# Local attention feeding a PReLU network: the first q in one load, later q and k behind it, and one weight split issued later

## The chip, the cores and the metric

The kernel runs on one core of a Trainium2 chip. The metric is the device time of one execution in microseconds (us); lower is better. The core has a matrix engine (PE; its weight loads are shown apart as PEld), a vector engine (DVE), a scalar engine (ACT), a general engine (POOL) and a queue engine (SP). Transfers are started by instructions on SP, ACT and POOL; the profile writes SPq, ACTq and POOLq where an engine only issues one. Each engine takes its instructions in a fixed order, and an instruction that waits holds up all that stand behind it on its engine.

## What is computed

Attention within chunks of 64 tokens, then a two-layer network with a PReLU, all in float32. The reference, cut to its core:

```python
# q, k, v: (8, 8, 576, 64); chunks of 64 tokens
scores = scale * np.matmul(q_c, k_c.transpose(0, 1, 2, 4, 3))
scores = scores - np.max(scores, axis=-1, keepdims=True)
attn = np.exp(scores)
attn = attn / (np.sum(attn, axis=-1, keepdims=True) + 1e-09)
out = np.matmul(attn, v_c)
# x: (4608, 512) from out; w_in: (512, 2048); w_out: (2048, 512)
h = x @ w_in
g = np.maximum(h, 0.0) + alpha * np.minimum(h, 0.0)
return (g @ w_out).astype(np.float32)
```

## The kernel before

**Tiling.** The 4608 tokens are 36 sub-blocks of 128 tokens (two chunks of 64, all eight heads). Four sub-blocks make a block of 512 tokens, so there are nine blocks. The first three blocks go through the network directly ("plain"); the other six go in three pairs through a scheme with seven half-size products in place of eight, whose combined weights are computed meanwhile and kept in DRAM.

**Number format.** Each float32 operand of the network is held as a high and a low part, and each product takes three passes: high by high, low by high, high by low. Weights reach the chip as raw words. `split_weight` (L120) turns one piece of a weight, 128 x 512, into its two parts: two instructions on ACT (the absolute value at L130, the rounded high part at L134) and seven on DVE (L131, L132, L133, L135, L136, L137, L138). There are 16 pieces of each weight; `wi[f]` belongs to the first layer and `wo[f]` to the second. `prepare(f)` (L141) splits both.

**Attention of an early sub-block s (the first eight).** It has three stages, called by `attend`:

- Stage 0: `attn_scores` multiplies q by a block-diagonal k on PE (L180); `attn_softmax` takes the maximum on DVE (L210), scales it (L211), forms eight exponentials on ACT, one for each head (L214, each an ACTIVATE and a read of its sum), and then on DVE the sum's reciprocal (L216, L217) and the product (L218).
- Stage 1: `attn_transpose` transposes the probabilities on PE (L242), and ACT copies them into a block-diagonal tile in two halves (L249, L250).
- Stage 2: `attn_values` multiplies by v on PE (L260), and `attn_x` writes the high part of the network's input x on ACT (L292) and its low part on DVE (L293).

Below, S, T and V with a number stand for the scores, the transposes and the values product of that sub-block, counted from 0.

**Network step.** `ffn_in` runs 12 matmuls of the first layer (L311) into one of two banks `ps_h`; `prelu` follows with L301 and L302 on ACT and L303 on DVE; L323 on ACT and L324 on DVE split the result into `gh` and `gl`; `ffn_out` runs 12 matmuls of the second layer (L336). The first three steps work on block 0 with weights 0, 1 and 2, the next nine on block 1 from weight 0 on, since the weights arrive one after the other. When a block's turn is over, `store` copies its sums out (L366).

**Order.** The instructions of the early part are put in order by a scheduler that estimates times; the kernel only gives priorities (`high_priority`) and orderings (`issue_after`: nothing inside may stand ahead of the instruction named). A small change to the program can therefore move instructions far behind it. From the 21st step on PE's own order is fixed by the program.

**Start.** `fetch("wi", 0)` loads the first weight piece on SP. `first_q(s, n, queue)` (L415) loads q of n sub-blocks, `first_k(s, other)` (L422) loads the two halves of a k, one on SP and one on the queue named, and `first_v` loads v of two sub-blocks. Several of the tiles carry names of weights (wi, wo), since they lie in rooms that later hold weights.

Of the kernel before, what the change touches and what calls it, by code (L numbers as in the profile page):

```python
# [18 lines left out]
def bits(pattern):  # L19
    return struct.unpack("f", struct.pack("I", pattern))[0]  # L20
# [7 lines left out]
def tile_local_attention_prelu_ffn(  # L28
# [12 lines left out]
    nc = tc.nc  # L41
# [31 lines left out]
    def f32(t):  # L73
        return t.bitcast(F32)
# [34 lines left out]
    wi, wo = {}, {}  # L109
# [4 lines left out]
    def fetch(side, f):  # L114
        name = ("raw", "raw", "more")[fetched[0] % 3]
        fetched[0] += 1
        raws[side, f] = stage.tile([P, 512], I64, name=name, bufs=2 if name == "raw" else 1)
        nc.sync.dma_start(out=raws[side, f], in_=(w_in if side == "wi" else w_out)[:, f])

    def split_weight(side, f):  # L120
        if (side, f) not in raws:
            fetch(side, f)
        raw = raws.pop((side, f))
        words = raw.bitcast(U32).rearrange("p (n two) -> p two n", two=2)
        low, high = words[:, 0], words[:, 1]
        t1 = stage.tile([P, 512], U32, name="t1")
        t3 = stage.tile([P, 512], U32, name="t3", bufs=1)
        w = const.tile([P, 2, 512], F32R, name=f"{side}{f}")
        hi, lo = w[:, 0], w[:, 1]
        nc.scalar.activation(f32(t1), f32(high), AF.Abs)  # L130
        nc.vector.tensor_scalar(f32(t1), f32(t1), bits(0x38000000), bits(0x47EFFFFF), op0=ALU.max, op1=ALU.min)  # L131
        nc.vector.tensor_scalar(t1, t1, 3, 0x3FFFF000, op0=ALU.logical_shift_left, op1=ALU.bitwise_and)  # L132
        nc.vector.scalar_tensor_tensor(t1, in0=high, scalar=0xC0000000, in1=t1, op0=ALU.bitwise_and, op1=ALU.bitwise_or)  # L133
        nc.scalar.copy(hi, f32(t1))  # L134
        nc.vector.tensor_scalar(t3, high, 0x1FF, 15, op0=ALU.bitwise_and, op1=ALU.logical_shift_left)  # L135
        nc.vector.scalar_tensor_tensor(t3, in0=low, scalar=17, in1=t3, op0=ALU.logical_shift_right, op1=ALU.bitwise_or)  # L136
        nc.vector.tensor_scalar(t1, t1, 0xFF800000, None, op0=ALU.bitwise_and)  # L137
        nc.vector.scalar_tensor_tensor(lo, in0=t3, scalar=2.0 ** -35, in1=f32(t1), op0=ALU.mult, op1=ALU.mult)  # L138
        return w

    def prepare(f, behind=None):  # L141
        with tc.issue_after(behind.ins) if behind else nullcontext():
            wi[f] = split_weight("wi", f)
            wo[f] = split_weight("wo", f)
# [7 lines left out]
    stages = {}  # L152
# [19 lines left out]
    def attn_scores(s):  # L172
        q_sb, kb, _ = qkv[s]
        early = s < EARLY
        if early:

            sc = attn_psum(s, 0)
            for h in range(H):
                par, hp = h % 2, h // 2
                pe(nc.tensor.matmul(  # L180
                    sc[par * C:(par + 1) * C, hp * P:(hp + 1) * P],
                    lhsT=q_sb[:, h, :],
                    rhs=kb[:, :, h],
                    start=True, stop=True,
                ))
            sc3 = sc.rearrange("p (g k) -> p g k", k=C)
        else:


            for hp in range(NP):  # L190
                for c in range(2):
                    for par in range(2):
                        rows = slice(par * C, (par + 1) * C)
                        pe(nc.tensor.matmul(  # L194
                            att[par][c * C:(c + 1) * C, (NP + hp) * C:(NP + hp + 1) * C],
                            lhsT=q_sb[rows, 2 * hp + c],
                            rhs=kb[rows, 2 * hp + c],
                            start=True, stop=True,
                        ))
            sc3 = [a[:, NP * C:].rearrange("p (g k) -> p g k", k=C) for a in att]  # L200
        return sc3

    def attn_softmax(s, sc3):
        early = s < EARLY
        mx = soft.tile([P, H, 1], F32, name="mx", bufs=2)
        pr = prs[s // 2 % 2][:, s % 2] if early else soft.tile([P, H, C], F32, name="pr")
        sm = soft.tile([P, H, 1], F32, name="sm", bufs=2)
        parts = [(slice(0, H), sc3)] if early else [(slice(b * NP, (b + 1) * NP), sc3[b]) for b in range(2)]
        for at, part in parts:
            nc.vector.tensor_reduce(mx[:, at], part, axis=AX.X, op=ALU.max)  # L210
        scaled = nc.vector.tensor_scalar(mx, mx, -SCALE, None, op0=ALU.mult)  # L211
        for g in range(H):
            one = sc3[:, g] if early else sc3[g // NP][:, g % NP]
            last = nc.scalar.activation(pr[:, g], one, AF.Exp, bias=mx[:, g], scale=SCALE, accum_out=sm[:, g])  # L214
        stages["softmax"] = scaled, last
        nc.vector.tensor_scalar(sm, sm, 1e-9, None, op0=ALU.add)  # L216
        nc.vector.reciprocal(sm, sm)  # L217
        nc.vector.tensor_tensor(pr, pr, sm.broadcast_to([P, H, C]), op=ALU.mult)  # L218
        probs[s] = pr
# [167 lines left out]
    def attend(part, s):  # L387
        with tc.high_priority(offset=HIGH):
            if part == 0:
                attn_softmax(s, attn_scores(s))  # L390
            elif part == 1:
                attn_transpose(s) if s < EARLY else attn_blocks(s)
            else:
                attn_x(s, attn_values(s))
# [20 lines left out]
    def first_q(s, n, queue):  # L415

        q_sb = qs[s // 2 % 2][:, s % 2:s % 2 + n]
        queue.dma_start(out=q_sb, in_=qT[:, s:s + n].rearrange("p s (h t) -> p s h t", t=C))
        for i in range(n):
            qkv[s + i] = [q_sb[:, i], kbds[(s + i) % NBD], None]  # L420

    def first_k(s, other):  # L422

        for c, queue in enumerate((nc.sync, other)):
            rows = slice(c * C, (c + 1) * C)
            queue.dma_start(out=kbds[s % NBD][rows, c], in_=kT[rows, s].rearrange("p (h t) -> p h t", t=C))
# [6 lines left out]
            qkv[s + i][2] = v_sb[:, i]  # L433

    fetch("wi", 0)
    first_q(0, 1, nc.scalar)
    first_k(0, nc.scalar)
    first_q(1, 1, nc.scalar)
    first_k(1, nc.scalar)
    first_q(2, 2, nc.sync)  # L440
    first_k(2, nc.sync)
    first_v(0)
    fetch("wo", 0)
# [1 line left out]
    first_v(2)  # L445
    fetch("wi", 1)
    nc.gpsimd.dma_start(out=alpha_sb, in_=alpha)
    prepare(0)
    ready = 1
    for i in range(SPB + 2):  # L450
        for st in range(2, -1, -1):
            if 0 <= i - st < SPB:
                attend(st, i - st)
                if st == 2 and i % 2:
                    first_q(i + 1, 2, nc.sync)
                    first_k(i + 1, nc.sync)
                    first_k(i + 2, nc.sync)
                    first_v(i + 1)
# [452 lines left out]
```

## Time and profile before

| | us |
|---|---|
| median of three runs | 839.68 |
| the three runs | 834.14, 841.08, 839.68 |
| the profiled execution, whole time | 837.25 |
| its span in the trace | 835.5 |
| PE busy in the span | 806.1 |
| first matmul of the network starts at | 37.54 |

The profiled execution's whole time is 1.75 us longer than its span. Times of day in the rows below count from the start of the span. A row of a timeline has start, duration, engine, line, operation, output tile, input tiles, shapes and count, and in square brackets the time for which the engine had stood idle and what ended that. In a timeline a run of instructions of one kind is merged; a score product of eight matmuls in the program shows as 16 there, since each is run as two.

### The profile page before, as it was taken

Reading aid. Unit: us, or ns where it says so; the run is one execution under the profiler, and the core shown is the slowest. Engines: PE = TensorE matmul, PEld = TensorE weight load, DVE = VectorE, ACT = ScalarE, POOL = GpSimd, SP = SyncE. Lnnn points to the kernel's source line nnn. Section 1 sums busy time; section 2 is a strip of 40 time slices with the busy share of each in tenths; the row PEclk is TensorE's granted clock in tenths of the full one; section 3 lists DMA queues with packets and bytes.
Section 4 is the critical chain, followed back from the end, with each engine's and each line's share of the span. In section 5 each row is a group of like instructions: output and inputs, shape, how many; then the busy total and the mean of one; then the engine's idle time right before and its main releaser. Section 6 shows DMA issues by size and latency. Waiting matters only on the chain.

```text
span 835.5 us, 15368 instructions
## 1 busy us (share of the span) xinstructions
PE 806.1 (96%) x5248; PEld 644.8 (77%) x5248; DVE 671.0 (80%) x1268; ACT 542.8 (65%) x1392; POOL 215.7 (26%) x340
## 2 busy tenths in 40 slices
PE   4799999999989899999999999999999999999998
PEld 3577888777768678787788788787887888888886
DVE  5899999979769888677688996777789966568875
ACT  5985666657666576677876555687765546566452
POOL 4006223224324432111112242111122422111232
PEclk9999999999999899999999999999999999999999
DMA  9629777656687868687876799786557995555788
GB/s 277 215 78 343 236 248 267 192 159 205 207 212 238 222 202 287 223 270 260 260 248 208 225 241 335 261 268 207 187 199 234 250 296 188 187 191 188 237 228 231
DMA packets 73966, 192.40 MB, mean 230 GB/s; under 512 B 11664, under 2 KB 19104, under 8 KB 73760
## 3 DMA queue, kind: packets, MB, share of 16 engines
q0 software_dynamic: 38272, 127.43, 48.7%
q1 hardware_dynamic: 27248, 48.91, 18.5%
q10 hardware_dynamic: 8368, 15.08, 5.6%
q8 instruction: 42, 0.69, 0.3%
q14 instruction: 36, 0.29, 0.1%
HBM read 135.27 MB, written 42.99 MB: 213 GB/s over the span
## 4 chain that ended last, share of the span: by engine, by line
PE 83%; ACT 4%; DMA 4%; DVE 3%; SPq 3%; issue 2%; ACTq 0%; POOL 0%; DVEq 0%
PE ps_o L623 19%; PE ps_o L756 15%; PE ps_h L756 12%; PE ps_h L311 12%; PE ps_o L336 12%; PE ps_h L623 9%; SPq L232 3%; DMA pT<-t 2%; PE ps_a L272 2%; PE ps_a L194 1%; DMA wi<-kT 1%; ACT wo L214 1%; ACT pr L214 1%; DMA wo_a<-raw 1%; ACT wi L214 1%
## 5 line engine op out<-in xcount | busy, mean ns | idle before, releaser
L336 PE MATMUL ps_o<-wo,gh 128*128 128x512 f32 x384 | 114.7, 397 | 1.2 <-ACT g L366 1.2
L311 PE MATMUL ps_h<-xh,wi 128*128 128x512 f32 x384 | 107.4, 402 | 1.8 <-DVE g L303 1.2
L311 PEld LDWEIGHTS ps_h<-xh,wi 128*128 128x128 f32 x384 | 72.0, 190 | 19.9 <-DVE g L303 1.7
L336 PEld LDWEIGHTS ps_o<-wo,gh 128*128 128x128 f32 x384 | 71.5, 188 | 19.1 <-ACT g L366 1.6
L214 ACT ACTIVATE pr<-ps_a,mx 128x64 f32<-128x64 f32 x224 | 67.3, 328 | 25.2 <-DVE mx L211 23.1
L336 PE MATMUL ps_o<-wo,gl 128*128 128x512 f32 x192 | 69.3, 396 | 0.1
L623 PE MATMUL ps_o<-wi,raw 128*128 128x512 f32 x171 | 67.9, 397 | 0.0
L623 PE MATMUL ps_o<-wo,raw 128*128 128x512 f32 x171 | 67.8, 396 | 0.0
L311 PE MATMUL ps_h<-xl,wi 128*128 128x512 f32 x192 | 53.4, 400 | 0.0
L561 POOL DMA_DIRECT2D raw<-wi_a x42 | 22.4, 532 | 106.4 <-PE ps_o L623 60.6
L214 ACT ACTIVATION_READ_ACCUMULATOR pr<-ps_a,mx 128x1 f32 x224 | 49.5, 221 | 0.0
L323 ACT CAST gh<-g 128x512 fp32r<-128x512 f32 x48 | 29.9, 622 | 28.9 <-DVE g L303 22.9
L301 ACT ACTIVATE wo<-gh 128x512 f32<-128x512 f32 x24 | 15.2, 634 | 50.4 <-DVE gh L646 50.4
L579 ACT CAST gh<-wi 128x512 fp32r<-128x512 f32 x45 | 28.1, 625 | 25.3 <-PE ps_o L756 10.3
L561 POOL DMA_DIRECT2D raw<-wo_a x42 | 22.4, 532 | 84.9 <-PE ps_o L756 44.0
L311 PEld LDWEIGHTS ps_h<-xl,wi 128*128 128x128 f32 x192 | 36.6, 191 | 8.7
L301 ACT ACTIVATE g<-ps_h 128x512 f32<-128x512 f32 x48 | 29.4, 613 | 21.1 <-PE ps_h L311 20.8
L336 PEld LDWEIGHTS ps_o<-wo,gl 128*128 128x128 f32 x192 | 35.9, 188 | 9.3 <-DVE gl L324 0.5
L623 PE MATMUL ps_o<-wi,wo 128*128 128x512 f32 x99 | 39.3, 397 | 0.0
L623 PE MATMUL ps_o<-wo,wo 128*128 128x512 f32 x99 | 39.1, 395 | 0.0
L623 PEld LDWEIGHTS ps_o<-wo,raw 128*128 128x128 f32 x171 | 32.2, 188 | 7.7
L623 PEld LDWEIGHTS ps_o<-wi,raw 128*128 128x128 f32 x171 | 32.1, 188 | 7.6
(251 smaller groups left out, 2285.3 us busy)
## 6 DMA issues: line engine op xcount, KB each, us to landing
raw<-wi_a POOLq DMA_DIRECT2D x42, 512.0 KB, 4.7
raw<-wo_a POOLq DMA_DIRECT2D x42, 512.0 KB, 4.7
wi<-wi_a POOLq DMA_DIRECT2D x21, 512.0 KB, 4.5
wo<-wi_a POOLq DMA_DIRECT2D x21, 512.0 KB, 4.7
wi<-wo_a POOLq DMA_DIRECT2D x21, 512.0 KB, 4.6
wo<-wo_a POOLq DMA_DIRECT2D x21, 512.0 KB, 5.1
v_sb<-v SPq DMA_DIRECT2D x28, 256.0 KB, 4.8
pT<-t SPq DMA_DIRECT2D x224, 32.0 KB, 4.0
```

Of the source, the lines that this page charges most:

```text
L194: pe(nc.tensor.matmul(att[par][c * C:(c + 1) * C, (NP + hp) * C:(NP + hp + 1) * C], lhsT=q_sb[rows, 2 * hp + c], rhs=kb[rows, 2 * hp + c], ...
L214: last = nc.scalar.activation(pr[:, g], one, AF.Exp, bias=mx[:, g], scale=SCALE, accum_out=sm[:, g])
L232: nc.sync.dma_start(out=pT[dst, i].rearrange("p h t -> p (h t)"), in_=tb[src, j].rearrange("p h t -> p (h t)"),)
L272: pe(nc.tensor.matmul(att[c][par * C:(par + 1) * C, hp * C:(hp + 1) * C], lhsT=v_sb[rows, h * C:(h + 1) * C], rhs=p[rows, :, par * NP + hp ...
L301: nc.scalar.activation(g, h, AF.Relu, scale=-1.0)
L311: pe(nc.tensor.matmul(hps, lhsT=wi[f][:, l, k * P:(k + 1) * P], rhs=xx[:, k], start=(i == 0 and k == 0), stop=(i == 2 and k == NK - 1),))
L323: nc.scalar.copy(gh, g)
L336: pe(nc.tensor.matmul(o, lhsT=a[:, ts], rhs=wo[f][:, l], start=(f == first and i == 0), stop=(f == last and i == 2),))
L561: streamed[0] = nc.gpsimd.dma_start(out=f32(t), in_=units[side][n])
L579: hi = nc.scalar.copy(t_hi, t)
L623: pe(nc.tensor.matmul(ps, lhsT=w[:, l, k * P:(k + 1) * P], rhs=xx[:, xl], start=first and at == 0, stop=at == n - 1, skip_group_check=not ...
L756: pe(nc.tensor.matmul(ps[m], lhsT=w[:, l, m * P:(m + 1) * P], rhs=xx, start=i != 6 and j == 0 and n == 0, stop=j == JF - 1 and n == 2, ski ...
```

## The change

Three calls at the start and one in the loop over the first block:

- The q of sub-blocks 0 and 1 come in one load of 512 KB on ACT's queue, ahead of both k's; before, there was a load of 256 KB, the first k's half, the second 256 KB and the second k's half.
- The q of sub-blocks 2 and 3 goes to ACT's queue behind these, and no longer to SP's queue ahead of the third k.
- `prepare(0)` is taken apart: `wi[0]` is split where it was, and `wo[0]` is split inside the loop, after the attention stage 0 of sub-block 2, and not ahead of the scaling of that sub-block's maximum.

```diff
     fetch("wi", 0)
-    first_q(0, 1, nc.scalar)
+    first_q(0, 2, nc.scalar)
     first_k(0, nc.scalar)
-    first_q(1, 1, nc.scalar)
     first_k(1, nc.scalar)
-    first_q(2, 2, nc.sync)
+    first_q(2, 2, nc.scalar)
     first_k(2, nc.sync)
     first_v(0)
     fetch("wo", 0)
...
-    prepare(0)
+    wi[0] = split_weight("wi", 0)
     ready = 1
     for i in range(SPB + 2):
         for st in range(2, -1, -1):
             if 0 <= i - st < SPB:
                 attend(st, i - st)
+                if st == 0 and i == 2:
+                    with tc.issue_after(stages["softmax"][0].ins):
+                        wo[0] = split_weight("wo", 0)
```

No instruction is added but for the merging: there is one load less. The scheduler's order changes on all engines, on PE, ACT and DVE far beyond the start. In the program of the changed kernel the lines behind the loop stand three lower; line numbers below 436 are the same in both.

At the start of ACT's program, with the two q tiles named wo_92 and wi_93, and the k tiles wo_84 and wi_85. Before:

```order
L418 DMA wo_92<-qT 128x512
L91 ACT_TABLE_LOAD
L91 ACTIVATE table<-table 128x1
L426 DMA wo_84<-kT 64x512
L418 DMA wo_92<-qT 128x512
L426 DMA wi_85<-kT 64x512
```

With the change:

```order
L418 DMA wo_92<-qT 128x1024
L91 ACT_TABLE_LOAD
L91 ACTIVATE table<-table 128x1
L426 DMA wo_84<-kT 64x512
L426 DMA wi_85<-kT 64x512
L418 DMA wi_93<-qT 128x1024
```

The second k's half now has 512 + 128 KB of its own queue ahead of it, which is what it had before (256 + 128 + 256 KB); the first k's half has 512 KB ahead of it where it had 256.

The second place is PE at the third network step, on which weight 2 is used (wo_640 before, wo_639 with the change). L242 on tile wi_95 is T7, and L260 on wi_91 is V7. Before:

```order
L336 MATMUL ps_o_674<-wo_520,gl 128x512
L242 MATMUL ps_a<-ident,wi_95 128x128 x4
L336 MATMUL ps_o_671<-wo_640,gh 128x512 x2
L336 MATMUL ps_o_672<-wo_640,gh 128x512 x2
L336 MATMUL ps_o_673<-wo_640,gh 128x512 x2
L336 MATMUL ps_o_674<-wo_640,gh 128x512 x2
L260 MATMUL ps_a<-wi_91,wi_97 64x128 x8
L336 MATMUL ps_o_671<-wo_640,gl 128x512
```

With the change:

```order
L311 MATMUL ps_h<-xh,wi_625 128x512 x4
L311 MATMUL ps_h<-xl,wi_625 128x512 x4
L311 MATMUL ps_h<-xh,wi_625 128x512 x4
L242 MATMUL ps_a<-ident,wi_95 128x128 x4
L260 MATMUL ps_a<-wi_91,wi_97 64x128 x8
L336 MATMUL ps_o_670<-wo_639,gh 128x512 x2
L336 MATMUL ps_o_671<-wo_639,gh 128x512 x2
```

The first-layer matmuls of this step stand directly ahead of T7, and V7 directly behind it; before, eight second-layer matmuls stood between T7 and V7.

The third place is ACT at the same step: L249 and L250 on tile wi_91 are the copies between T7 and V7, and L301 and L302 the step's PReLU. Before:

```order
L301 ACTIVATE g<-ps_h 128x512
L292 CAST xh<-ps_a 128x4x128
L130 ACTIVATE t_703<-raw 128x512
L302 ACTIVATE g<-g,alpha_sb 128x512
L323 CAST gh<-g 128x512
L249 COPY wi_91<-ps_a 64x512
L250 COPY wi_91<-ps_a 64x512
```

With the change:

```order
L301 ACTIVATE g<-ps_h 128x512
L302 ACTIVATE g<-g,alpha_sb 128x512
L130 ACTIVATE t_702<-raw 128x512
L249 COPY wi_91<-ps_a 64x512
L250 COPY wi_91<-ps_a 64x512
L134 CAST wi_690<-t_688 128x512
L323 CAST gh<-g 128x512
```

The two copies still stand behind the step's L301 and L302, and now ahead of its L323.

## The prediction

> **What bounds the kernel now.** I read the page first (span, busy time, slices), then busy time by windows, then the chain of waits of the first 70 us, then the timeline around the places that the new order touches.
>
> ```profile
> span 835.5 us, 15368 instructions
> PE 83%; ACT 4%; DMA 4%; DVE 3%; SPq 3%; issue 2%; ACTq 0%; POOL 0%; DVEq 0%
> 20.00:30.00 10.00, 7.17 (x75) 5.61 (x73) 7.96 (x20) 9.93 (x48) 0.00 (x0) 0.83 1.04 306
> 30.00:40.00 10.00, 6.38 (x65) 5.04 (x66) 7.47 (x20) 9.93 (x44) 0.00 (x0) 1.00 0.50 168
> 70.00:80.00 10.00, 10.00 (x45) 8.08 (x44) 9.97 (x20) 4.62 (x9) 5.09 (x8) 1.00 1.01 370
> 130.00:180.00 50.00, 50.00 (x273) 39.98 (x272) 46.27 (x100) 32.70 (x80) 13.17 (x16) 1.00 0.60 194
> 280.00:330.00 50.00, 46.65 (x362) 37.26 (x363) 42.80 (x91) 34.29 (x111) 16.04 (x23) 0.93 0.77 250
> ```
>
> A window's row has the stretch, its length, the busy time of PE, PEld, DVE, ACT and POOL, the granted clock, the DMA share and GB/s. PE carries 83% of the last chain, and from 70 us on it is full but for a few gaps. From 20 to 40 us ACT is the full engine (9.93 of 10). So what happens before PE's first network matmul counts as far as it shortens ACT's chain, and later only a change of PE's gaps counts.
>
> ```profile
> 2.69 8.66 DMA wi<-kT
> 11.49 1.99 PE ps_a L180 x16
> 14.50 2.47 ACT wo L214 x16
> 16.97 0.58 ACT t L130
> 18.59 2.47 ACT wi L214 x16
> 25.85 0.45 ACT wo L249
> 26.31 0.58 ACT wo L250
> 37.54 2.13 PE ps_h L311 x8
> ACT wo L214 <- DVE mx L211: 3.1, 2, 2.6
> 9.46 0.31 ACT L214 ACTIVATE wo<-ps_a,mx 128x64 f32<-128x64 f32 x1 [0.53 <-DVE mx L211]
> 15.46 0.43 DVE L135 TENSOR_SCALAR t<-raw 128x512 uint32<-128x512 uint32 x1 [0.22 <-DMA raw<-w_out]
> 17.25 0.17 DVE L211 TENSOR_SCALAR mx<-mx 128x8 f32<-128x8 f32 x1
> ```
>
> The chain of waits says it: the second k's half, issued at 2.69, lands 8.66 us later; S1 runs at 11.49, the second softmax at 14.50, the third at 18.59, and PE's first L311 at 37.54. Between the first softmax and the second, ACT waits 2.6 us for that k.
>
> **The change part by part, to the first L311.** (a) The k of sub-block 1. It has the same 640 KB ahead of it on its queue as before, but the 512 KB of the next q no longer compete from the other queue. It needs to land 2.5 us earlier for the wait to vanish. S1 cannot run before S0 has ended, which is 2 us after S0's start, so I take it that it lands in time, between 8 and 10 us. (b) The price: S0 now waits for 512 + 128 KB on ACT's queue where it had 256 + 128. Nothing shows that load alone; the bounds are 0 (the 256 KB beyond hide behind the first weight) and 1.5 us (they take their share of a rate of some 300 GB/s with two queues: 0.85 us alone, twice that at half rate). I take 0.4, and another 0.4 since in the new order L137 (0.43, as L135) stands between the first L210 and its L211. The first softmax then runs 10.25 to 12.75 and the second right behind it to 15.25, against 16.97 + 0.03 before: 1.7 us gained. (c) The split of `wo[0]`. All nine instructions move: seven on DVE, whose L135 and L136 stood ahead of the third maximum, and two on ACT. The third maximum was ready at 17.4 and ACT got to it at 18.59, so DVE's part was covered and its going yields nothing. On ACT L130 stays directly behind the second softmax. It needs `w_out`, which landed at 15.46; the bytes ahead of it are the same in sum, but SP now holds the second half of the third k until the first q's load is counted, and `w_out` stands behind it. Bounds: 15.0 and 16.9; I take 15.9. So the third softmax starts at 15.9 + 0.58 + 1.1 (the pair L249, L250) = 17.6, a gain of 1.0. (d) The rest of ACT's chain. Counting the rows of the order from the third softmax to the L292 that releases L311: before 32 exponentials, with the change 36 (2.47 / 8 = 0.31 each: +1.24), one L134 more (+0.6), one pair L249, L250 less (0.45 + 0.58: -1.03). That is +0.8, and ACT has no idle time here to hide it. First L311: 37.54 - 1.0 + 0.8 = 37.3, so -0.2 of the 2.6 us waited for; the bounds from (b) and (c) are 36.4 and 38.1.
>
> **The change, from there to 70 us.** Here the order moved PE's work, and I followed it by hand at 0.233 us a matmul (four take 0.93 in the rows below).
>
> ```profile
> 43.43:47.40 3.97, 3.97 (x39) 2.63 (x37) 3.97 (x9) 3.91 (x8) 0.00 (x0) 1.00 0.28 83
> 52.53 0.64 ACT L301 ACTIVATE g<-ps_h 128x512 f32<-128x512 f32 x1
> 54.05 0.77 ACT L302 ACTIVATE g<-g,alpha_sb 128x512 f32<-128x512 f32 x1
> 56.15 0.63 ACT L323 CAST gh<-g 128x512 fp32r<-128x512 f32 x1 [1.33 <-DVE g L303]
> 57.09 0.60 PE L242 MATMUL ps_a<-ident,wi 128*128 128x128 f32 x4
> 57.45 2.11 PE L336 MATMUL ps_o<-wo,gh 128*128 128x512 f32 x8
> 57.73 0.58 ACT L249 COPY wi<-ps_a 64x512 f32<-64x512 f32 x1 [0.96 <-PE ps_a L242]
> 58.32 0.58 ACT L250 COPY wi<-ps_a 64x512 f32<-64x512 f32 x1
> 59.49 1.09 PE L260 MATMUL ps_a<-wi,wi 128*64 128x128 f32 x16
> 60.52 1.20 PE L336 MATMUL ps_o<-wo,gl 128*128 128x512 f32 x4
> 61.55 0.62 PE L311 MATMUL ps_h<-xh,wi 128*128 128x512 f32 x2
> 64.34 1.10 PE L311 MATMUL ps_h<-xh,wi 128*128 128x512 f32 x4
> 65.28 1.10 PE L311 MATMUL ps_h<-xl,wi 128*128 128x512 f32 x4
> 68.47 1.21 PE L311 MATMUL ps_h<-xh,wi 128*128 128x512 f32 x4 [1.16 <-DVE g L303]
> ```
>
> (e) V4 moves behind the first 24 L311 (1.05, as V7's pace of 59.49 to 60.52), T5 ahead of them (0.4): +0.6 behind the first L311. The mixed stretch of T6, S7 and V5, 3.97 us before, stays. (f) T7 and V7. Before, T7 ended at 57.45, and while ACT copied (57.73 to 58.90) PE ran eight L336; V7 followed at 59.49 without a wait and `gh` was there in time (L323 at 56.15). With the change all twelve L311 of weight 2, T7 and V7 stand in a row, and on ACT the step's L301, L302 and an L130 stand ahead of the two copies. From the end of those L311: 0.60 + 0.65 + 0.58 + 0.58 + 0.58 = 3.0 us until V7 may start (durations of the rows, the first two less some 0.1 by which ACT's instructions overlap), with 0.4 of T7 as the only work beside it: PE stands 2.6 us. The first term of that sum cannot start early, since L301 needs the last of the twelve. `gh` is ready when V7 ends (L134 and L323 on ACT, 1.1, beside V7's 1.05). Before, T7's start to the next L311 was 4.46; now 0.4 + 2.6 + 1.05 + 12 x 0.233 = 6.85: +2.4. The bounds are 0, if ACT's queue is so far ahead that only the copies are left, and 3.0. (g) The wait of 1.16 for L303 at 68.47 comes again, since L301 again stands behind the four copies of L366; PE arrives later, so I take 0.8 of it: -0.4.
>
> Sum: -0.2 + 0.6 + 2.4 - 0.4 = +2.4 us at about 70 us. From there PE was full to 180 us (50.00 of 50 in the last stretch) and the shift stays. DVE is full too (9.97 of 10), but the same splits are done in the same total, and PE now needs them later.
>
> **The scale.** Against the profiled execution's own 837.25 the sum gives 839.65; that execution was 2.43 below the median of 839.68. The four executions known differ by 6.94 us and have a mean of 838.04, which is the fairest base: 838.04 + 2.4 = 840.4, rounded to 840.5. About 1% (8.4 us) is what a measurement of this kernel can tell from no change.
>
> **What lies between 180 and 330 us.** The chain leaves PE there, and ACT's and DVE's order is changed up to about 310 us, so this is the widest unknown.
>
> ```profile
> 19.44:22.85 3.41, 1.26 (x18) 0.88 (x16) 2.46 (x8) 3.41 (x18) 0.00 (x0) 1.00 1.04 272
> 22.85:26.27 3.42, 3.42 (x30) 2.76 (x27) 2.47 (x7) 3.38 (x16) 0.00 (x0) 0.50 1.07 313
> 33.10:36.50 3.40, 1.55 (x30) 1.31 (x28) 2.67 (x8) 3.36 (x19) 0.00 (x0) 1.00 0.45 140
> 282.27:285.68 3.41, 0.57 (x4) 0.19 (x2) 2.96 (x8) 3.41 (x18) 0.00 (x0) 1.00 0.98 335
> 285.68:292.50 6.82, 6.31 (x72) 5.29 (x73) 5.88 (x13) 2.25 (x5) 2.90 (x4) 0.50 0.64 192
> 284.64 0.33 PE L272 MATMUL ps_a<-pT,v_sb 64*64 64x64 f32 x2 [2.12 <-ACT xl L288]
> 286.19 1.02 PE L272 MATMUL ps_a<-pT,v_sb 64*64 64x64 f32 x27 [1.23 <-DVE raw L537]
> ```
>
> PE stood 2.12 + 1.23 = 3.35 us there, and behind it the granted clock was 0.50 for 6.82 us, which costs half of that, 3.4. One such event is 6.8 us. The likeliest is that it stays.
>
> **The rivals.**
>
> - *The gap at T7 trips the clock.* A window of 3.41 us with 1.26 us of PE work was followed by 0.50, one with 1.55 was not. A gap of 2.6 leaves 0.8 if it lies in one window. Price: 1.7 for one window at half clock, 3.4 for two: 842.2 to 843.9, on the slower side. It decides where the gap falls against the windows: over 2.1 of its 2.6 us must lie in one.
> - *The start's gain arrives.* If k lands as said and V7 finds its copies done (the lower end of f), the sum is -0.2 + 0.6 - 0.4 = 0.0, and with L311 at 36.4 another 0.9 less: 837.1. For it speaks the wait of 2.6 us, which does end; against it, that L301 is ahead of the copies in ACT's order.
> - *A second event as at 284 us*, at another attention visit: 840.4 + 6.8 = 847.2, slower.
> - *The event at 284 us is gone*, since ACT's and DVE's rows stand otherwise there: 840.4 - 6.8 = 833.6, faster.
> - *The change doesn't do what it says:* k lands as late as before, with the second softmax at 14.5 and S0 0.8 later; then (a) gives nothing, L311 starts at 38.3 and the time is 841.4, inside the range.
>
> On the first rival the Trainium skill has a rule, in "TensorE: Matmul & The Clock Gate", Part 1 on the clock gate: the clock halves after at least one idle window of about 3.4 us, on a window that runs free. By that rule a gap of 2.6 us would cost nothing beyond itself. This trace agrees for 282.27:285.68, but at 19.44:22.85 PE worked 1.26 us and the clock still halved, so the measurement keeps the rival alive.
>
> **Chances.** My forecast 0.45; clock tripped 0.15; gain arrives 0.15 (with half of it still within 1 us of no change); second event 0.10; event gone 0.12; no earlier k 0.03. The range takes all of these in, from 833.0, below the event gone, to 847.0, just short of the second event, whose upper half it leaves out with what lies beyond both ends: about 0.2. Faster by over 1% (below 831.3) needs the event gone and the gain: 0.04. Slower by over 1% (above 848.1) needs the second event and the clock: 0.06. The rest, 0.90, is within 1%.
>
> **What would show it.** Right on (a): the second softmax on ACT directly behind the first, with no wait for L211. Right on (c): L130 with a short wait for `w_out`, the third softmax at 17.6. Right on (d): first L311 at 36.4 to 38.1. Right on (f): a PE wait at V7 (L260) for ACT's L250 of 2 to 3 us near 58 us. Wrong: that wait absent; a first L311 before 36; PE idle in 280 to 330 us that differs from 3.35 by more than 2, or another number of stretches at half clock.

## The result, and the profile after

The changed kernel takes 843.5 us (median of 11 runs, 840.37 to 846.58), the kernel before 838.73 us (11 runs, 834.14 to 841.92). The ratio is 1.006, with a 95% interval from 1.0044 to 1.0075: slower by about 5 us, less than the 1% that the prediction took as the bound of "no change". Forecast were 840.5 us, with a range from 833 to 847. The profiled executions differ by 6.2 us in their spans (841.7 against 835.5); the terms below are made against that difference. One execution of each kernel is profiled, and the times of these two kernels spread over 6 to 8 us, so a term of a microsecond in one trace can be chance.

The chain of waits of the changed kernel, first to the first `L311`, answers to the first block of rows in the prediction (start, length, what).

```profile
1.25 6.14 DMA wo<-kT
7.53 3.70 PE ps_a L180 x32
11.22 1.40 ACT wo L214 x9
12.69 3.39 ACT wo L214 x22
16.07 0.32 ACT t L130
16.42 0.62 ACT wo L249
17.66 2.39 ACT wi L214 x15
37.29 6.73 PE ps_h L311 x24
```

The wait of 2.6 us between the first two softmaxes is gone: S0 and S1 run as one piece on PE (32 matmuls from 7.53), and ACT works from 11.22 on without a wait worth naming. Yet PE's first `L311` starts at 37.29, against 37.54 before. The stretch that was freed is filled with other work of ACT, as forecast.

Now PE in the timeline of the changed kernel (start, length, line and operation, number of matmuls; in brackets the idle time ahead and its releaser):

```profile
37.29 3.01 PE L311 MATMUL ps_h<-xh,wi 128*128 128x512 f32 x8 [0.39 <-ACT xh L292]
43.95 1.09 PE L260 MATMUL ps_o<-wo,wo 128*64 128x128 f32 x16
56.12 1.09 PE L311 MATMUL ps_h<-xh,wi 128*128 128x512 f32 x4
58.92 0.60 PE L242 MATMUL ps_a<-ident,wi 128*128 128x128 f32 x4
62.20 1.10 PE L260 MATMUL ps_a<-wi,wi 128*64 128x128 f32 x16 [2.68 <-ACT wi L250]
63.36 3.58 PE L336 MATMUL ps_o<-wo,gh 128*128 128x512 f32 x8
67.70 2.02 PE L311 MATMUL ps_h<-xh,wi 128*128 128x512 f32 x8
75.02 1.19 PE L311 MATMUL ps_h<-xh,wi 128*128 128x512 f32 x4 [1.57 <-DVE g L303]
```

V7 (62.20) waits 2.68 us for its two copies. ACT in the timeline, from the end of weight 2's `L311` to those copies, shows the chain that the prediction added up to 3.0 us:

```profile
59.18 0.60 ACT L301 ACTIVATE g<-ps_h 128x512 f32<-128x512 f32 x1 [1.97 <-PE ps_h L311]
59.81 0.72 ACT L302 ACTIVATE g<-g,alpha_sb 128x512 f32<-128x512 f32 x1
60.44 0.65 ACT L130 ACTIVATE t<-raw 128x512 f32<-128x512 f32 x1
60.99 0.56 ACT L249 COPY wi<-ps_a 64x512 f32<-64x512 f32 x1
61.56 0.58 ACT L250 COPY wi<-ps_a 64x512 f32<-64x512 f32 x1
```

The eight `L336` behind V7 take 3.58 us, where they took 2.11 before; and already the first eight `L311` take 3.01 instead of 2.13. The windows of the changed kernel tell why (stretch, its length, busy time of PE, PEld, DVE, ACT and POOL, granted clock, DMA share, GB/s):

```profile
29.02:32.44 3.42, 1.41 (x23) 1.24 (x25) 3.38 (x9) 3.38 (x16) 0.00 (x0) 1.00 0.59 235
32.44:35.85 3.41, 2.34 (x19) 1.64 (x15) 2.51 (x7) 3.41 (x19) 0.00 (x0) 0.50 0.69 184
35.85:39.26 3.41, 3.02 (x9) 2.24 (x10) 1.55 (x3) 3.37 (x17) 0.00 (x0) 0.50 0.35 129
59.75:63.16 3.41, 0.96 (x16) 0.85 (x16) 2.36 (x5) 3.34 (x7) 0.00 (x0) 1.00 0.20 41
63.16:66.58 3.42, 3.36 (x12) 2.54 (x9) 3.42 (x9) 1.96 (x4) 0.19 (x1) 0.50 0.36 132
244.07:247.48 3.41, 1.08 (x41) 0.87 (x45) 3.38 (x7) 2.02 (x5) 1.46 (x2) 1.00 1.06 348
```

PE ran at half clock from 32.44 to 39.26, over the first `L311`, and from 63.16, right behind the gap at V7. Each of these stretches follows a window with little PE work (1.41 and 0.96 us). So in this execution the first rival of the prediction (the gap trips the clock) came true, and a stretch at half clock over the first `L311`, for which the prediction had no term, came with it. The last row is a window of the later stretch, behind which half clock follows too.

**Where the time went.** PE's work from its first `L311` on is nearly the same in every kernel here (119.0 to 121.8 us up to the first visit, but for e4 with its added matmuls), so a shift in time can be added up from four parts: the start of the first `L311`, PE's idle time behind it, the loss to half clock, and the work. Two rows each, first of the kernel before and then of the changed kernel, from the first `L311` to the first late visit (the first `L194`) and from there to the fifteenth:

```profile
37.54:157.98 120.44, 119.28 (x556) 94.95 (x556) 114.20 (x236) 81.08 (x163) 33.97 (x44) 1.00 0.69 229
157.98:343.73 185.75, 179.38 (x1538) 141.81 (x1540) 153.89 (x329) 123.50 (x393) 60.24 (x82) 0.98 0.70 210
```

```profile
37.29:164.53 127.24, 122.92 (x568) 97.70 (x568) 115.91 (x237) 81.21 (x156) 34.75 (x44) 0.98 0.65 216
164.53:348.53 184.00, 177.83 (x1537) 140.96 (x1540) 154.42 (x325) 123.52 (x393) 59.57 (x81) 0.99 0.68 210
```

Idle is the length less PE's busy time. The loss to half clock is the length times what the granted clock lacks to 1, summed over pieces of 0.4 us (the two digits of the rows are too coarse for it). The work is what remains.

| us | before | changed | difference |
|---|---|---|---|
| start of the first `L311` | 37.54 | 37.29 | -0.25 |
| to the first visit: idle | 1.16 | 4.31 | +3.15 |
| to the first visit: half clock | 0.00 | 2.69 | +2.69 |
| to the first visit: work | 119.28 | 120.24 | +0.96 |
| first visit | 157.98 | 164.53 | +6.55 |
| to the 15th visit: idle | 6.36 | 6.16 | -0.20 |
| to the 15th visit: half clock | 3.41 | 1.71 | -1.70 |
| to the 15th visit: work | 175.98 | 176.13 | +0.15 |
| 15th visit | 343.73 | 348.53 | +4.80 |
| from there to the end of the span | 491.8 | 493.2 | +1.4 |

The whole loss is made between 37 and 158 us. The work is longer by V4, which now lies behind the first `L311` instead of ahead of it, less T5, which now lies ahead (568 records against 556). Between the visits the changed kernel wins back 1.7 us, since it has one window at half clock there instead of two. That one is not half of the old pair: the event at 284 us is gone, and another, a wait of 2.33 us for a k at 247.33, has come with half clock behind it. The half clock over the first `L311` cannot be put down to the change. Up to that matmul PE's order in e1, e3, e4 and e10 below is the changed kernel's, and in e6, e8, e11 and e12 the kernel before's. Half clock reaches over the first `L311` in four of the five traces with the one order and in three of the five with the other (e6, e11 and e12); in the kernel before's own trace the window ahead, 33.10:36.50 in the prediction, escaped with 1.55 us of work. So 0.98 of the 2.69 may come from which executions were profiled.

The last stretch took between 491.8 and 493.7 us in all but one of the profiled executions of this study (499.1 in that one, e4), whatever was changed ahead of it, so I put its 1.4 down to the execution.

### The profile page after: what moved, and what is told of

Same layout as the page of the kernel before. It is cut to its first block, busy times and chain, and to the rows that moved or that the text cites. A ratio compares the mean times of both kernels' runs of the same rounds, so it can differ in the third digit from the quotient of the medians.

```text
span 841.7 us, 15365 instructions
## 1 busy us (share of the span) xinstructions
PE 808.5 (96%) x5248; PEld 646.1 (77%) x5248; DVE 674.2 (80%) x1268; ACT 543.6 (65%) x1392; POOL 216.1 (26%) x340
## 4 chain that ended last, share of the span: by engine, by line
PE 75%; DMA 8%; ACT 7%; DVE 4%; SPq 2%; issue 2%; ACTq 0%; POOL 0%; DVEq 0%
PE ps_o L759 15%; PE ps_o L626 15%; PE ps_h L311 12%; PE ps_o L336 12%; PE ps_h L759 11%; PE ps_h L626 7%; DMA v_sb<-v 3%; SPq L232 2%; DMA pT<-t 2%; ACT pr L214 2%; PE ps_a L272 1%; ACT wo L214 1%; DMA wi<-wo_a 1%; PE ps_a L194 1%; DMA wo<-kT 1%
## 5 line engine op out<-in xcount | busy, mean ns | idle before, releaser
L336 PE MATMUL ps_o<-wo,gh 128*128 128x512 f32 x384 | 117.6, 404 | 0.1
L311 PE MATMUL ps_h<-xh,wi 128*128 128x512 f32 x384 | 106.4, 401 | 3.4 <-DVE g L303 3.0
L311 PEld LDWEIGHTS ps_h<-xh,wi 128*128 128x128 f32 x384 | 71.9, 190 | 21.5 <-DVE g L303 3.8
L336 PEld LDWEIGHTS ps_o<-wo,gh 128*128 128x128 f32 x384 | 73.3, 192 | 18.0 <-ACT gh L323 0.3
L336 PE MATMUL ps_o<-wo,gl 128*128 128x512 f32 x192 | 70.4, 398 | 0.2 <-DVE gl L324 0.2
L311 PE MATMUL ps_h<-xl,wi 128*128 128x512 f32 x192 | 52.8, 395 | 0.0
L301 ACT ACTIVATE wo<-gh 128x512 f32<-128x512 f32 x24 | 15.2, 634 | 50.8 <-DVE gh L649 50.8
L323 ACT CAST gh<-g 128x512 fp32r<-128x512 f32 x48 | 29.8, 621 | 24.8 <-DVE g L303 22.2
L336 PEld LDWEIGHTS ps_o<-wo,gl 128*128 128x128 f32 x192 | 36.4, 189 | 9.7 <-DVE gl L324 1.0
L311 PEld LDWEIGHTS ps_h<-xl,wi 128*128 128x128 f32 x192 | 36.1, 188 | 8.6
L301 ACT ACTIVATE g<-ps_h 128x512 f32<-128x512 f32 x48 | 29.4, 613 | 19.0 <-PE ps_h L311 18.8
L324 DVE TENSOR_TENSOR gl<-g,gh 128x512 fp32r<-128x512 f32 x48 | 32.8, 686 | 6.6 <-ACT gh L323 5.3
```

The source lines that it names most:

```text
L301: nc.scalar.activation(g, h, AF.Relu, scale=-1.0)
L311: pe(nc.tensor.matmul(hps, lhsT=wi[f][:, l, k * P:(k + 1) * P], rhs=xx[:, k], start=(i == 0 and k == 0), stop=(i == 2 and k == NK - 1),))
L323: nc.scalar.copy(gh, g)
L324: low = nc.vector.tensor_tensor(gl, g, f32(gh), op=ALU.subtract)
L336: pe(nc.tensor.matmul(o, lhsT=a[:, ts], rhs=wo[f][:, l], start=(f == first and i == 0), stop=(f == last and i == 2),))
```

## The experiments

Each was timed in five rounds beside the kernel before, which took 838.69 us beside e1 to e4, 837.29 beside e5 to e8 (on another chip) and 837.79 beside e9 to e12; the ratios are against these. In the table "first visit" is the shift against the kernel before's 157.98 us; idle and half clock, from the one trace of each, are those between the first `L311` and the first visit. e1 to e5, e7, e9 and e10 have all or part of the change; e6, e8, e11 and e12 have its loads and its split not at all.

| kernel | us | ratio, 95% interval | first `L311` | idle | half clock | first visit |
|---|---|---|---|---|---|---|
| before | 838.73 | | 37.54 | 1.16 | 0.00 | |
| changed | 843.5 | 1.006 (1.0044 to 1.0075) | 37.29 | 4.31 | 2.69 | +6.55 |
| e1 loads only | 843.04 | 1.0047 (1.003 to 1.0064) | 37.73 | 4.29 | 2.70 | +6.99 |
| e2 split only | 844.39 | 1.0071 (1.0056 to 1.0085) | 36.57 | 5.61 | 1.71 | +7.75 |
| e3 cover | 852.07 | 1.0159 (1.0141 to 1.0176) | 36.86 | 3.02 | 2.81 | +5.45 |
| e4 filler | 843.72 | 1.0072 (1.0045 to 1.0099) | 36.43 | 3.05 | 1.04 | +5.97 |
| e5 next q only | 840.24 | 1.003 (1.0013 to 1.0047) | 38.34 | 3.10 | 1.66 | +4.52 |
| e6 row alone | 846.48 | 1.011 (1.0086 to 1.0133) | 36.26 | 5.95 | 3.42 | +6.78 |
| e7 warm start | 844.45 | 1.0086 (1.0053 to 1.0119) | 36.18 | 7.09 | 3.41 | +8.87 |
| e8 visit later | 838.01 | 1.0009 (0.9994 to 1.0025) | 37.00 | 1.19 | 0.00 | -0.41 |
| e9 V4 first | 842.03 | 1.0047 (1.0028 to 1.0065) | 40.42 | 1.43 | 2.09 | +5.37 |
| e10 hold earlier | 842.41 | 1.0057 (1.0037 to 1.0076) | 36.90 | 4.49 | 1.71 | +5.56 |
| e11 before, hold later | 841.97 | 1.0048 (1.0032 to 1.0065) | 37.65 | 4.11 | 0.98 | +4.62 |
| e12 before, hold earlier | 840.93 | 1.0048 (1.0027 to 1.0069) | 37.28 | 4.65 | 2.37 | +5.37 |

**e1, loads only.** The changed kernel with the split put back.

```
 first_q(0, 2, nc.scalar); both k's; first_q(2, 2, nc.scalar)   (as changed)
-wi[0] = split_weight("wi", 0)
+prepare(0)
...
-with tc.issue_after(stages["softmax"][0].ins):
-    wo[0] = split_weight("wo", 0)
```

> The three loads as in the changed kernel, both splits of weight 0 as before. Theory A (the time went into the row of L311, T7 and V7 without cover, and into the half clock behind it; this order comes with the loads): the order on PE from V4 to the second block is the changed kernel's word for word, so V7 waits 2 to 3 us near 60 us, a half-clock window follows, and the time is 842 to 845. Theory B (the moved split of the second weight costs the time): 837 to 840, no V7 wait over 1 us.

Measured: 843.04 us. V7 waits 2.67 us at 62.64, and half clock follows. The third softmax starts at 18.11, 0.45 later than with the split moved too. Theory A holds here, B falls: the loads alone bring the order and the loss. PE's order is the changed kernel's to the end of the kernel.

**e2, split only.** The changed kernel with the loads put back.

```
-first_q(0, 2, nc.scalar); both k's; first_q(2, 2, nc.scalar)
+first_q(0, 1, nc.scalar); first_k(0); first_q(1, 1, nc.scalar); first_k(1); first_q(2, 2, nc.sync)
 wi[0] = split_weight("wi", 0)   (and wo[0] behind the third maximum, as changed)
```

> Loads as before, only the split of the second weight behind the third maximum. S0 again at 6.5 us, the second softmax again at 14.5. Theory A: here too T7 and V7 stand in a row behind the last four L311 of weight 2, so V7 waits 2 to 3 us and the time is 840.5 to 843. Theory C (S0's delay by the loads is what costs): 836 to 839.

Measured: 844.39 us, 1.4 above what A gave and far above C. S0 runs at 6.59 and the second softmax at 14.43, as before the change, and still V7 waits 2.72 us at 62.83. So each half of the change costs as much as both together; the two do not add up. The gap is as long as the changed kernel's, but no half clock follows. The windows of e2 show the difference, which is where the gap falls:

```profile
57.77:61.18 3.41, 2.19 (x11) 1.36 (x9) 3.19 (x8) 1.75 (x4) 0.00 (x0) 1.00 0.37 135
61.18:64.60 3.42, 1.77 (x19) 1.52 (x20) 3.38 (x7) 3.36 (x8) 0.00 (x0) 1.00 0.48 153
64.60:68.01 3.41, 3.41 (x16) 2.74 (x16) 3.41 (x8) 0.55 (x2) 2.59 (x5) 1.00 0.31 77
```

Here it is shared by two windows, and each keeps 1.77 us of PE work or more; in the changed kernel one window held nearly all of it and kept 0.96.

**e3, cover.** The second layer of weight 1 is held behind the first layer of weight 2, so that its twelve `L336` stand ahead of T7 and V7.

```
+stages["h"] = ...   (the last L311 issued; in ffn_in)
-second(*pending.pop(0))
+with tc.issue_after(stages["h"].ins) if n == 2 else nullcontext():
+    second(*pending.pop(0))
```

> The changed kernel, with the second-layer matmuls of weight 1 held behind the first-layer matmuls of weight 2, so that these twelve L336 (2.8 us) stand ahead of T7 and V7. Theory A: V7's wait falls from 2.68 to under 0.7, no half-clock window at 60 to 70 us, and the time falls by 2 to 4.3, to 839 to 841.5. Theories B, C and D (loss in the loads or after 180 us): 842.5 to 844.5.

Measured: 852.07 us, the slowest of all. At the place itself A holds in part: V7's wait falls to 1.26, no half clock follows it, and block 1's first `L311` comes at 66.49 instead of 67.70, although 1.8 us more were lost to half clock at the first `L311` of all. But at 256 us PE waits 7.27 us, and 2.53 more at 261, for the copies of `L366`, for which no other kernel waits more than 1.8 us at once. PE in the timeline of e3:

```profile
256.32 1.22 PE L336 MATMUL ps_o<-wo,gh 128*128 128x512 f32 x2 [7.27 <-ACT more L366]
```

The edit touched nothing there; the order of ACT and DVE after it did. Why that copy came so late was not followed up.

**e4, filler.** Ten matmuls that compute nothing of the output (they are overwritten) stand between T7 and V7.

```
 xo = attn_psum(s, 2)
+if s == EARLY - 1:
+    with tc.issue_after(stages["T"].ins):
+        for _ in range(10):
+            nc.tensor.matmul(xo, lhsT=wi[0][:, 0, :P], rhs=x[0][0][:, 0], start=True, stop=True)
```

> The changed kernel with ten idle 128x512 matmuls (2.33 us at full clock) between T7 and V7, written to the bank that V7 overwrites. It prices the clock apart from the wait. If the gap trips the clock: 63 to 67 us stays at full clock, V7 starts as late as before the filler (62.2), the eight L336 behind it take 2.0 instead of 3.58, and the time is 1.0 to 2.0 lower, 841.5 to 842.5. If the half clock there has another cause: the window stays at 0.50 and the time is 843 to 845.

Measured: 843.72 us, no gain that can be told from none. The record at the place is what was expected if the gap trips the clock. PE in the timeline of e4, whose lines behind 258 are four further down:

```profile
58.13 0.60 PE L242 MATMUL ps_a<-ident,wi 128*128 128x128 f32 x4
58.48 2.58 PE L261 MATMUL ps_a<-xh,wi 128*128 128x512 f32 x10
61.41 1.09 PE L264 MATMUL ps_a<-wi,wi 128*64 128x128 f32 x16 [0.35 <-ACT wi L250]
62.58 2.13 PE L340 MATMUL ps_o<-wo,gh 128*128 128x512 f32 x8
```

From T7's start to V7's are 3.28 us, just as without the filler (58.92 to 62.20), and the eight matmuls behind take 2.13 instead of 3.58. So half clock there costs about 1.45 over these eight. That the gap brings it is not shown by this trace alone, since e2 has the same gap and no half clock; the count of windows in the last section shows it. By the first visit that gain is gone: PE waits 0.67 at 84.75 and 0.58 at 96.76, which the changed kernel does not. Its profiled execution (850.29) is the slowest of its six and lost 5 us more between 421 and 510 us than the changed kernel's; only its front is read here.

**e5, the next q only.** The kernel before with one edit: `first_q(2, 2, nc.sync)` becomes `first_q(2, 2, nc.scalar)`.

> The kernel before, with one edit of the change: only the load of q of the third and fourth sub-blocks goes behind both k's on ACT's queue; the first two q's stay two loads, both splits of weight 0 as before. Theory A (S0's delay of 1.07 us is the size of the first q load): S0 starts again at 6.3 to 6.7 us, k of the second sub-block still lands before 10.5, so the second softmax starts 1 to 2.5 us before the 14.5 of the kernel before. T7 and V7 stand behind nine L336 and four L311, so V7 waits under 1.5. Time 836 to 841. Rival (S0's delay comes from the shared queue, whichever load is longer): S0 at 7.2 to 7.8.

Measured: 840.24 us; the profiled execution (844.61) is the slowest of its twelve. S1 starts at 9.37 and the second softmax at 13.2, 1.3 ahead of the kernel before, so taking the next q from SP's queue is enough to have the second k nearly in time. S0 starts at 7.03, between the two figures, so the size of the first load is neither shown nor excluded as the cause of its delay. V7 waits 1.26. A third of the change's parts thus costs about half of its time.

**e6, the row alone.** The kernel before, with weight 2's first layer held behind weight 1's second layer.

```
+stages["o"] = ...   (the last L336 issued; in ffn_out)
+if n == 2:
+    second(*pending.pop(0))
-pending.append((acc, ffn_in(x[b], f), ...))
+with tc.issue_after(stages["o"].ins) if n == 2 else nullcontext():
+    pending.append((acc, ffn_in(x[b], f), ...))
```

> The kernel before, loads and splits untouched, with the first-layer matmuls of weight 2 held behind the second-layer matmuls of weight 1, as they stand in the changed kernel; so T7 and V7 follow them in a row. It prices the order alone. Theory A: V7 waits 2 to 3.3 us near 60 us, PE reaches the first visit (158 us in the kernel before) 2 to 5 us later, by the larger figure where a half-clock window follows; the time is 841 to 844. If the loads or the moved split cost the time by themselves: no change at the first visit over 1 us, and 837.5 to 839.5.

Measured: 846.48 us, 2.5 above the range given. PE in the timeline of e6:

```profile
59.38 1.09 PE L260 MATMUL ps_a<-wi,wi 128*64 128x128 f32 x16 [1.36 <-ACT wi L250]
61.83 2.12 PE L311 MATMUL ps_h<-xh,wi 128*128 128x512 f32 x8 [1.34 <-ACT xh L292]
73.72 1.61 PE L311 MATMUL ps_h<-xh,wi 128*128 128x512 f32 x4 [3.25 <-DVE g L303]
```

V7 waits less than said (1.36), but block 1's first `L311` waits for V7's x (1.34), and the third step for L303 (3.25, with half clock behind it). An edit to the order, without a byte moved, makes the whole loss and more; the orders of PE, ACT and DVE are the kernel before's up to 47 us and differ behind that. Of its 3.41 us of half clock 1.7 lie at the first `L311`, ahead of the edit. So order alone can cost this much; where its wait is charged varies.

**e7, warm start.** The changed kernel with ten such filler matmuls behind T3, where PE waited 3.03 us for S6.

```
+if s == 6:
+    warm = ps_h.tile([P, TB], F32, name="ps_h")
+    with tc.issue_after(stages["T", 3].ins):
+        (ten matmuls of wi[0] on wi[0] into warm)
```

> The changed kernel with ten idle 128x512 matmuls (2.33 us) behind the fourth transpose group, in the 3.03 us in which PE waited for ACT before S6 at 31.03. From the windows seen so far a window with less than about 1.55 us of matmul work is followed by half clock. Theory A: no half clock over the first L311, the first eight L311 take 2.1 instead of 3.0, PE reaches the first visit 0.7 to 1.7 earlier than the changed kernel's 164.5; the T7 wait of 2.7 stays; 841.5 to 843. Rival: the window at half clock stays, since PE had work in that window already; 843 to 845.

Measured: 844.45 us; A falls. The filler took the wait (0.73 left ahead of S6), but the window that tripped the clock was another one, from 32.85 to 36.27, with 1.41 us of PE work, and the first eight first-layer matmuls took 3.66. Then a wait of 3.05 at 84.25 came, with half clock behind it. V7 waited 2.53, this time without half clock.

**e8, a visit later.** In the kernel before, the list of late visits has 81 in place of 80, so that twelve `L311` stand ahead of the visit that waited 2.12 and 1.23 us.

> The kernel before, with the twelfth late visit of the attention moved from ahead of a first-layer step to behind it (80 to 81 in the list), so twelve L311 (2.8 us) stand ahead of the matmuls that waited 2.12 and 1.23 us at 284 to 286 us. Theory A (that event costs its idle time and the half clock behind it): the waits shrink to under 1.2 together, no half-clock window at 286 to 293, 3 to 6.8 us less: 832 to 836. Rival (ACT and DVE are late by more than the matmuls cover, or the next visit waits instead): 837 to 840.

Measured: 838.01 us, the same as before; A falls and the rival holds. That visit waits 1.12 now, the next ones 0.66, 0.95 and 0.73, with half clock at 310 us; another half-clock window came at 249 us, behind waits for `L366`. Against the kernel before PE stands at +1.27 at the twelfth visit, -3.02 at the thirteenth and +0.63 at the fifteenth. In this stretch ACT and DVE are behind, and PE's wait moves to wherever cover ends.

**e9 to e12: who holds weight 2 back.** By then a theory (H) had come up on why the changed kernel's weight 2 is late. `prepare` holds the split of weight 2 behind `done_x[SPB]`, the low part of sub-block 4's x (`L293` of V4). DVE in the timeline, before and then changed:

```profile
40.95 0.69 DVE L293 TENSOR_TENSOR xl<-ps_o,xh 128x512 fp32r<-128x512 f32 x1
41.55 0.42 DVE L131 TENSOR_SCALAR t<-t 128x512 f32<-128x512 f32 x1
```

```profile
46.43 0.68 DVE L293 TENSOR_TENSOR xl<-ps_o,xh 128x512 fp32r<-128x512 f32 x1
47.02 0.42 DVE L131 TENSOR_SCALAR t<-t 128x512 f32<-128x512 f32 x1
```

The split's first DVE operation follows `L293` at once in both. V4 stood ahead of the first `L311` before and stands behind 24 of them now, so the split starts 5.5 us later, and weight 2's `L311` come at 56.12 instead of 47.40, behind all the `L336` that could have covered its chain.

```
e9   +with tc.issue_after(stages["V", SPB].ins) if n < 2 else nullcontext():   (around ffn_in; changed kernel)
e10  -{2: SPB, 3: SPB + 2, ...}  +{2: SPB - 1, 3: SPB + 2, ...}   (changed kernel)
e11  -{2: SPB, 3: SPB + 2, ...}  +{2: SPB + 1, 3: SPB + 2, ...}   (kernel before)
e12  -{2: SPB, 3: SPB + 2, ...}  +{2: SPB - 1, 3: SPB + 2, ...}   (kernel before)
```

> The changed kernel with V4 held ahead of the first L311, as in the kernel before. The theory by now (call it H): the split of weight 2 is held behind the low part of sub-block 4's x (L293 of V4). The change put V4 behind 24 L311, so that split starts 5.5 us later (L131 at 47.0 instead of 41.55), weight 2's L311 come at 56.1 instead of 47.4, and nothing is left to cover its chain L301, L302, L303, L323 and the copies for V7. By H: the first L311 some 0.5 to 1.5 later than 37.3, V7's wait under 0.7, no half clock at 60 to 67, PE reaches the first visit at 158 to 161 (changed kernel 164.5), time 836.5 to 840.5 if nothing new comes after 180 us. Rival (the loads, or V4's place as such): the first visit at 163 or later, 842 to 845.

> The changed kernel with one number changed: the split of weight 2 is held behind the low part of sub-block 3 instead of 4. V4 stays behind the 24 L311. By H: weight 2's split starts before V4's L293, its L311 run ahead of the L336 of weights 0 and 1, V7 waits under 0.7, no half clock behind it, the first visit at 158.5 to 161.5, time 837 to 841 if nothing new comes after 180 us. Rival (V4's late place itself, or the loads): the first visit at 163 or later, 842 to 845.

> The kernel before, untouched loads and splits, with the split of weight 2 held behind sub-block 5 instead of 4. It makes that split late without the change. By H: weight 2's L311 behind the L336 of weight 1, V7 waits 1.5 to 3 us near 60 us, the first visit 2 to 6.5 us later (160 to 164.5), time 840 to 845. Rival: no more than 1 us at the first visit, 837 to 839.

> The kernel before with the split of weight 2 held behind sub-block 3 instead of 4; a candidate to beat both kernels. By H the kernel before has no uncovered wait at T7 and V7, so little is to be had there: the first visit within 1 us of 158, time 836 to 838.5. It would be slower if the earlier split takes DVE and ACT from the attention's chain ahead of the first L311 (first L311 later than 38): 839 to 841.

Measured for e9: 842.03 us. The split starts at 42.20, V7 has no wait that the profile shows, and the idle time to the first visit falls to 1.43: the mechanism is as said. But V4 waits 2.48 us for its copies, so the first `L311` starts at 40.42 (said: at most 38.8), and it runs at half clock. What was saved at V7 was paid at the start; the time is above the 840.5 given.

Measured for e10: 842.41 us. The split starts at 37.48, and V7 waits only 0.34. But with the `L336` used up ahead of V7, block 1's first `L311` has nothing ahead of it while ACT copies V7's x. PE in the timeline of e10:

```profile
64.94 1.62 PE L311 MATMUL ps_h<-xh,wi 128*128 128x512 f32 x4 [2.50 <-ACT xh L292]
```

Half clock follows there as well. PE reaches the first visit 1.0 us earlier than in the changed kernel, not 3 to 6 as said.

Measured for e11: 841.97 us, in the range given, and the first visit 4.62 later; but V7 waits only 0.34, though the split starts at 50.34 (the wait of 1.38 is again block 1's first `L311`). Measured for e12: 840.93 us, where 836 to 838.5 was said: the earlier split makes the kernel before slower too, with 1.94 of wait at block 1's first `L311` and 2.72 at the third step.

So the first half of H is shown in one direction: with an earlier split of weight 2 V7's wait goes (e9, e10). A late split alone does not bring it (e11), so it also takes the rest of the changed order. The second half of H, that the time comes back with the wait, is refuted. Nothing that was tried beats the kernel before; e8 equals it.

## Why the prediction was right and where it was wrong

- **(a) The second k lands in time.** Right. S1 runs directly behind S0, and the second softmax directly behind the first; e5, with a wait of 0.36 us left ahead of S1, shows that the q on the other queue was nearly all of it.
- **(b) The price at S0.** Mis-sized: +1.07 in this pair of executions, against the 0.4 taken. Over all executions with the merged load S0 starts at 7.05 to 7.53 (seven of them, mean 7.24), with the first q alone and the next q on SP at 6.44 to 6.92 (six, mean 6.68): 0.56, inside the bounds of 0 and 1.5. The first weight on the other queue is late too: DVE's first use of it is at 5.60 to 6.42 in these seven and at 5.04 to 5.48 in the six. That fits the upper bound's reason, that the larger load takes its share of the rate. The first softmax starts 1.76 later than before, where the sum had 0.8: DVE is still at the late first weight when S0 ends.
- **(c) The third softmax.** It starts at 17.66, and 17.6 was said, but partly by luck: the wait for `w_out` that the sum contains did not come, since S0's delay pushed ACT's work past it. e1 prices the split's move at 0.45 us here.
- **(d) First `L311`.** 37.29, forecast 37.3. That the 2.6 us would not arrive there was right, and the reason holds: from the third softmax to there ACT is busy for 19.49 of 19.63 us. The agreement to 0.01 us is luck. With the kernel before's order of PE up to there, five traces start at 36.26 to 37.65, and with the changed order five start at 36.43 to 37.73.
- **(e) V4 behind the `L311`.** As PE work it was priced about right (+0.6, where the record has +0.96 for all of PE's work up to the first visit). What it left out is that V4 also releases the split of weight 2, which is 5.5 us late through it. With an earlier split V7's wait goes (e9, e10), and a later split alone does not bring it (e11). The row itself the prediction had read off the order, so its cost stood in (f).
- **(f) The gap at V7.** The mechanism was right: the wait is 2.68, forecast 2.6. From T7 to the next `L311` it took 8.78, and the sum had 6.85; nearly all of the rest is the half clock behind the gap (1.71). The rival that names it gave 842.2 to 843.9, and the time is 843.5. Its chance of 0.15 was too low by the prediction's own numbers: a gap of 2.6 us that trips the clock if 2.1 of it lie in one window of 3.41 does so for (2.6 + 3.41 - 2 x 2.1) / 3.41 = 0.53 of the positions. Of the four executions with this gap (changed, e1, e2, e7) two had half clock behind it.
- **(g) L303.** The wait came again, but as 1.57 instead of 0.8: +0.4 instead of -0.4.
- **The step of the sum that failed: half clock at nothing.** At 75.02, behind L303's wait, PE is already 6.55 us later than before (68.47), and the sum had +2.4. Of the 4.15 between them 2.69 are half clock: 0.98 over the first `L311`, for which there was no term though the prediction's own rows at 19.44 and 22.85 show such a window in the stretch ahead of it, and 1.71 behind V7, which stood among the rivals and not in the sum. (g) is 0.8; 0.7 is spread over smaller differences. That the forecast time lies only 3 us below the measured one is partly luck, since the stretch between the visits gave 1.75 us back.
- **Between the visits.** "Stays" came out nearly right in the total of idle time (-0.20) and off by one window of half clock (-1.70), but not in kind. In 280 to 330 us PE's idle time is 2.86 instead of 3.35 and no window is at half clock, which by the prediction's own sign counts against it. The rival "the event is gone" came true there, and a smaller event at 247 us with shorter waits behind it paid most of it back. e8 shows the same: the wait moves to another visit when it is closed at one.

Shown by the runs: the loss lies between the first `L311` and the first visit, as idle time and half clock, and a changed order is enough to bring it (e6, e11 and e12 have a loss of that size with the loads untouched, e1 and e2 each bring it alone). Ten of the eleven experiments that alter the order of that stretch have 3.0 to 7.1 us of idle time there; only e9 comes near the kernel before's 1.16, and pays at the start. Open is whether an order exists that keeps this cover and the earlier second softmax; it was not tried to hold all of the kernel before's order with the new loads, so what the loads alone would cost or gain in that order is not shown. Open too is how far the larger first load explains S0's delay: e5, with the small one, has S0 at 7.03.

## What to carry to other kernels

Where a scheduler sets the order, price a small change to the start by the order that comes out of it: the 2.6 us that the loads freed were never seen by PE, while a V4 that slid behind 24 matmuls also held back the next weight's split. When an instruction moves, look up who is held behind it, and not only how long it lasts. Before closing a wait, look at what is left to cover the next one: here V7's wait, once closed, came back at block 1's first `L311`.

## What the hardware showed that was not expected

The granted clock goes by windows of 3.413 us that run through the whole execution, and a window need not be idle to trip it. In each of the fourteen traces the edges of all stretches at half clock up to 360 us lie on one such grid to 2 ns. I laid it over that time, from the first row of the clock that a trace has (10.5 to 20.2 us). Of the 1351 windows at full clock, all 39 with up to 1.53 us of PE busy time are followed by half clock, none of the 1299 with over 1.73; of the 13 between, 6 are. Of the 57 windows at half clock, the 12 with up to 2.90 us busy (1.45 at full clock) are followed by another, the 45 from 2.92 up by full clock. So about 1.5 us of full-clock work in 3.41, or 45%, decides.

Ahead of that first row the views print a granted clock of 1.00, but PE ran at half clock there. The sixteen matmuls of the first scores take 1.97 to 1.98 us in all fourteen traces; the same sixteen take 1.09 at full clock, as in the changed kernel:

```profile
7.53 1.98 PE L180 MATMUL ps_a<-wo,wo 128*64 128x128 f32 x16 [7.53 <-DMA wo<-kT]
13.80 1.09 PE L180 MATMUL ps_a<-wo,wi 128*64 128x128 f32 x16 [2.60 <-ACT wo L214]
```

Read as half clock, the windows ahead of the first row keep the same limit with one exception in 55: 41 of the 42 with under 2.90 us busy are followed by another at half clock, the 13 with more by full clock.

The Trainium skill says in "TensorE: Matmul & The Clock Gate", Part 1, that the clock halves after at least one idle window of about 3.4 us and that the window runs free. The length and the free run agree with these traces; "idle" does not, since a window with up to 1.5 us of work counts. Nor does 282.27:285.68, which the prediction took as agreeing: with 0.57 us of work it is not an idle window. It follows from the free run that the same gap costs 1.7 us in one execution and nothing in the next, as in the changed kernel and e2.
